# RetNet attention and a bilinear feed-forward: the last block of rows, its groups one after the other, its sums in PSUM banks of their own

## The chip, the cores and the metric

The kernel runs on one core of a Trainium2 chip, as one launch. The metric is the device time of that launch in microseconds (us); lower is better. Before the change three runs took 321.66, 322.04 and 322.22 us; their median is 322.04 us.

## The reference

Eight batches of eight heads, 576 positions, head size 64. Each head's scores are damped by a power of its own gamma, without a softmax, and multiplied into the values. The heads are then laid side by side, which gives 4608 rows of 512 numbers, and a bilinear feed-forward layer follows: two products to 1536 columns, multiplied with each other, and a product back to 512 columns.

```python
scores = scale * (q @ k.T)                       # per batch and head, 576 x 576
D[i, j] = gamma[h] ** (i - j) if i >= j else 0
x = ((scores * D) @ v)                           # heads side by side: 4608 x 512
out = ((x @ w_a) * (x @ w_b)) @ w_out            # 1536 wide inside, 4608 x 512 float32 out
```

## The kernel before, in words

The rows go through the feed-forward in blocks: one of 512, two of 256, and then seven of 512 (`blocks`, L127). The attention of later rows is woven between the matmuls of earlier blocks by a list of jobs with due times (`todo`). By the last block all attention is done; nothing is woven into it but its own work.

For a block of 512 rows, `ffn_block` (L1064) runs twelve steps, one for each 128 of the 1536 inner columns. A step makes `pa` with four matmuls (L1090), ScalarE copies it to `ha` in bf16 (L1101), TensorE makes `pb` with four matmuls (L1108), and VectorE multiplies the two into `hT` (L1113). `row_sums` (L944) then makes sums of pieces of `hT` on VectorE (L952), partly into `hsum` and partly in place.

From row 1536 on, the product with `w_out` is done by `rows_mixed` (L982), with seven products in place of eight of the two-by-two blocks (a scheme of Strassen's kind). A block has two groups of 256 rows, g = 0 and 1. For each group there are seven "ways" of six matmuls (128x256 outputs, L1009), 84 matmuls in a block. The results of one group are gathered from four PSUM areas:

- `straights[g]`: way 3, later with way 6 added, in its first half; way 4, later with way 7 added, in its second half.
- `both[:, g]`: way 1. `crosses[g]`: ways 5 and 2.

Vector work puts them together. `kept("straight", ...)` and `kept("crossed", ...)` are copies on ScalarE (L1019). GpSimd adds the two copies into the middle half of the output tile `osb` (L1038). VectorE makes `less` = way 1 minus `crossed` (L1045), and after ways 7 and 6 it adds `less` to the two halves of `straights[g]`, which gives the outer quarters of `osb` (L1054, two adds of 256 columns for each group).

TensorE takes its instructions in the order in which the program writes them. Before, that is: ways 3 and 4 for both groups, way 1 for both, ways 5 and 2 for group 0, then for group 1, ways 7 and 6 for group 0, then for group 1. `straights[0]`, `straights[1]` and the cross area of group 1 come from the four-bank pool `ps_ffn`; way 1 of both groups and the cross area of group 0 share one two-bank tile `m15`.

The stores: in all blocks but the last they are put off to the next block (`formed`, `store_formed`) and issued by the SP queue. The last block (`closing`) cannot put them off. Its group 0 holds leftover rows of four batches, so `store_mixed` (L959) issues four transfers for it, of 32 tile rows of 4 KB each; they go to the ACT queue. Its group 1 is one piece of 128 tile rows, stored in three parts by the SP queue: the middle half after GpSimd (256 KB), and each outer quarter after its add (128 KB each).

Of the kernel before, what the change touches and what calls it, by code (L numbers as in the profile page):

```python
# [10 lines left out]
FP32 = mybir.dt.float32  # L11
# [3 lines left out]
ALU = mybir.AluOpType  # L15
# [3 lines left out]
def kernel(  # L19
# [10 lines left out]
    nc = tc.nc  # L30
# [14 lines left out]
    NP = NTOK // 256  # L45
# [16 lines left out]
    def place(n):  # L62
        return n if n < NP - 2 else 2 * NP - 3 - n

    def rows_of(n):

        if n not in LEFT:
            b, m = PAIRS[n]
            return [(kp, 0, 128, b, 256 * m + 128 * kp) for kp in (0, 1)]
        return [(i // 2, 64 * (i % 2), 64, 4 * LEFT[n] + i, S - 64)  # L70
                for i in range(4)]

    def pool(name, bufs, space=None):
        kw = {} if space is None else {"space": space}
        return ctx.enter_context(tc.tile_pool(name=name, bufs=bufs, **kw))
# [13 lines left out]
    late, early = {}, ExitStack()  # L89
# [13 lines left out]
    ps_ffn = pool("ps_ffn", 4, PS)  # L103
    opening, ps_sc, ps_o = ExitStack(), {}, {}
# [155 lines left out]
    def pair_tables(step):  # L260
# [6 lines left out]
        else:  # L267
            for h in (2 * step - 2, 2 * step - 1):
# [8 lines left out]
                for n in range(FIRST)]  # L277
    second = sum_pool.tile([128, FIRST, HP, 64], FP32, tag="sums",
                           name="second")
# [28 lines left out]
    def work(budget, up_to=2):  # L308
        jobs.sort(key=lambda job: job[0])
        while jobs and jobs[0][0] <= up_to and jobs[0][1] <= budget:  # L310
            _, cost, job = jobs.pop(0)
            job()
            budget -= cost

    def pass_on(count):
        while copies_due and count:
            copies_due.pop(0)()
            count -= 1
# [610 lines left out]
    WIDE = DM // 2  # L929
# [29 lines left out]
    def store_mixed(G, osb, cols=slice(0, 2 * DM), on=nc.sync):  # L959

        n = place(G)
        for kp, r0, m, b, s0 in rows_of(n):
            if n in LEFT:
                p0 = kp * 64 + r0 // 2
                m //= 2
            elif kp == 1:
                continue
            else:
                p0, m = 0, 128
            rows = out[b * S + s0:b * S + s0 + 2 * m].rearrange(  # L970
                "(p two) c -> p (two c)", two=2)
            on.dma_start(rows[:, cols],
                              osb[p0:p0 + m].rearrange("p k c -> p (k c)")
                              [:, cols])

    formed = []
# [5 lines left out]
    def rows_mixed(tok0, hT, sums):  # L982

        pass_on(math.inf)
        NP2 = NF // 2
        pair = [tok0 // 256 + g for g in (0, 1)]
        closing = NP - 1 in pair
        straights = [ps_ffn.tile([128, 2, WIDE], FP32, tag="ab",
                                 name=f"m34{g}") for g in (0, 1)]
        mixed = ps_o[0].tile([128, 2, 2, WIDE], FP32, tag="o", name="m15")  # L990
        apart = ps_ffn.tile([128, 2, WIDE], FP32, tag="ab", name="m52")
        both, crosses = mixed[:, 0], (mixed[:, 1], apart)

        def product(g, way, ps, begins=True):
            t0 = 256 * g
            to = {1: both[:, g], 2: crosses[g][:, 1], 3: straights[g][:, 0],
                  4: straights[g][:, 1], 5: crosses[g][:, 0],
                  6: straights[g][:, 0], 7: straights[g][:, 1]}[way]
            for p in ps:
                even, odd = 2 * p, 2 * p + 1  # L1000
                rows, cols = {
                    1: (sums[:, 0, p, g], wo_sums[:, 0, p]),
                    2: (hT[:, even, t0 + 128:t0 + 256], wo_sb[:, even, 0:WIDE]),
                    3: (hT[:, even, t0:t0 + 128], wo_sums[:, 3, p]),
                    4: (hT[:, odd, t0 + 128:t0 + 256], wo_sums[:, 4, p]),
                    5: (hT[:, odd, t0:t0 + 128], wo_sb[:, odd, WIDE:]),
                    6: (sums[:, 1, p, g], wo_sums[:, 1, p]),
                    7: (sums[:, 2, p, g], wo_sums[:, 2, p])}[way]
                nc.tensor.matmul(to, rows, cols, start=(begins and p == 0),  # L1009
                                 stop=True, skip_group_check=True)  # L1010
                yield 0.5, False

        osbs = [o_pool.tile([128, 2, DM], FP32, tag="osb", name="osb2")
                for _ in pair]
        flats = [osb.rearrange("p k m -> p (k m)") for osb in osbs]

        def kept(name, own):
            t = late[name].tile([128, 2, WIDE], FP32, tag=name, name=name)
            nc.scalar.copy(t, own)  # L1019
            return t  # L1020

        first, rest = range(NP2 - 1), (NP2 - 1,)
        for part in (first, rest):
            for g in (0, 1):
                yield from product(g, 3, part)
                yield from product(g, 4, part, False)
        kept_straight = [kept("straight", straights[g]) for g in (0, 1)]
        for part in (range(4), range(4, NP2)):
            for g in (0, 1):
                yield from product(g, 1, part, g == 0)  # L1030
        work(math.inf)
        pass_on(math.inf)
        lesses = []
        for g in (0, 1):
            yield from product(g, 5, range(NP2))
            yield from product(g, 2, range(NP2), False)
            crossed = kept("crossed", crosses[g])
            nc.gpsimd.tensor_tensor(  # L1038
                flats[g][:, WIDE:3 * WIDE].rearrange("p (k m) -> p k m", k=2),
                crossed, kept_straight[g], op=ALU.add)  # L1040
            if pair[g] == NP - 1:
                store_mixed(pair[g], osbs[g], slice(WIDE, 3 * WIDE))
            less = late["less"].tile([128, 2, WIDE], FP32, tag="less",
                                     name="less")
            nc.vector.tensor_tensor(  # L1045
                less, both[:, g].unsqueeze(1).to_broadcast([128, 2, WIDE]),
                crossed, op=ALU.subtract)
            lesses.append(less)
        for g in (0, 1):
            yield from product(g, 7, range(NP2), False)  # L1050
            yield from product(g, 6, range(NP2), False)
            for k, at, i in ((1, slice(0, WIDE), 0),
                             (0, slice(3 * WIDE, 4 * WIDE), 1)):
                nc.vector.tensor_tensor(flats[g][:, at], straights[g][:, k],  # L1054
                                        lesses[g][:, i], op=ALU.add)
                if pair[g] == NP - 1:
                    store_mixed(pair[g], osbs[g], at)
            if closing and pair[g] < NP - 1:
                store_mixed(pair[g], osbs[g], on=nc.scalar)
            elif not closing:  # L1060
                formed.append((pair[g], osbs[g]))
        yield 0, True

    def ffn_block(tb, tok0, n, runs):  # L1064
# [62 lines left out]
        if tok0 >= 256 * MIXED:  # L1127
            yield from rows_mixed(tok0, hT, sums)
            return
# [119 lines left out]
    starts, at = {}, 0.0  # L1249
# [89 lines left out]
    at = 0.0  # L1339
# [40 lines left out]
```

## Time and profile before

| | us |
|---|---|
| median of three runs | 322.04 |
| the profiled execution, whole | 322.96 |
| its span, first to last instruction | 321.0 |
| TensorE busy | 312.6 (97% of the span) |
| VectorE busy | 199.7 (62%) |
| ScalarE busy | 145.6 (45%) |
| GpSimd busy | 155.7 (49%) |
| chain that ended last, share on TensorE | 92% |

The profile is one execution of the program. A line of a timeline has the start, the duration, the engine, the line of the kernel, the operation and the tiles; a bracket behind it tells how long the engine sat idle before it and what ended that. PE is TensorE, DVE VectorE, ACT ScalarE, POOL GpSimd; SPq and ACTq are the queues of SyncE and ScalarE that issue transfers. "us to landing" of a transfer runs from its issue to the arrival of its completion. All clock times below are us from the start of the span.

### The profile page before, as it was taken

Reading aid. Unit: us, or ns where it says so; the run is one execution under the profiler, and the core shown is the slowest. Engines: PE = TensorE matmul, PEld = TensorE weight load, DVE = VectorE, ACT = ScalarE, POOL = GpSimd, SP = SyncE. Lnnn points to the kernel's source line nnn. Section 1 sums busy time; section 2 is a strip of 40 time slices with the busy share of each in tenths; the row PEclk is TensorE's granted clock in tenths of the full one; section 3 lists DMA queues with packets and bytes.
Section 4 is the critical chain, followed back from the end, with each engine's and each line's share of the span. In section 5 each row is a group of like instructions: output and inputs, shape, how many; then the busy total and the mean of one; then the engine's idle time right before and its main releaser. Section 6 shows DMA issues by size and latency. Waiting matters only on the chain.

```text
span 321.0 us, 9165 instructions
## 1 busy us (share of the span) xinstructions
PE 312.6 (97%) x3799; PEld 184.3 (57%) x3799; DVE 199.7 (62%) x374; ACT 145.6 (45%) x323; POOL 155.7 (49%) x169
## 2 busy tenths in 40 slices
PE   8999999999999999999999999999999999999992
PEld 3554457768544554548554864476447744764482
DVE  4845347767758563489558854875667566744652
ACT  6745346536435463454464625553436343323330
POOL 3990078564995577573895099408950300030011
PEclk9999999999999999999999999999999999999998
DMA  8999999999989999999999979974330300030004
GB/s 213 255 200 207 256 228 193 183 209 182 196 176 221 223 218 186 233 219 261 199 251 229 172 233 157 178 170 153 73 65 2 133 3 0 2 122 11 1 0 131
DMA packets 144793, 50.92 MB, mean 159 GB/s; under 512 B 126576, under 2 KB 141680, under 8 KB 144752
## 3 DMA queue, kind: packets, MB, share of 16 engines
q1 hardware_dynamic: 138224, 44.84, 70.2%
q0 software_dynamic: 5808, 4.72, 9.4%
q10 hardware_dynamic: 720, 0.79, 0.9%
q8 instruction: 29, 0.48, 0.7%
q14 instruction: 12, 0.10, 0.1%
HBM read 37.75 MB, written 9.44 MB: 147 GB/s over the span
## 4 chain that ended last, share of the span: by engine, by line
PE 92%; DVE 4%; ACT 1%; issue 1%; DVEq 0%
PE pb L1108 29%; PE pa L1090 28%; PE m L1009 15%; PE po L1134 8%; PE w L1159 2%; PE po L913 2%; PE o L744 1%; PE sc L703 1%; PE o L731 1%; PE kv L632 1%; DVE hT L952 1%; PE tp L373 1%; DVE sums L659 1%; DVE hsum L952 1%; PE sc L391 1%
## 5 line engine op out<-in xcount | busy, mean ns | idle before, releaser
L1113 DVE TENSOR_TENSOR hT<-ha,pb 128x512 bf16<-128x512 bf16 (+1 forms) x120 | 75.7, 632 | 79.5 <-PE pb L1108 67.8
L1108 PE MATMUL pb<-xT,wb_sb 128*128 128x512 bf16 (+1 forms) x480 | 111.6, 358 | 0.1
L1090 PE MATMUL pa<-xT,wa_sb 128*128 128x512 bf16 (+1 forms) x472 | 109.9, 358 | 0.0
L1101 ACT CAST ha<-pa 128x512 bf16<-128x512 f32 (+1 forms) x120 | 64.9, 542 | 97.2 <-PE pa L1090 94.7
L1108 PEld LDWEIGHTS <-wb_sb 128*128 128x128 bf16 x480 | 46.8, 98 | 47.6 <-issue 1.9
L1090 PEld LDWEIGHTS <-wa_sb 128*128 128x128 bf16 x472 | 45.0, 98 | 43.1 <-issue 0.2
L1038 POOL TENSOR_TENSOR osb<-crossed,straight 128x512 f32<-128x512 f32 x12 | 15.2, 1271 | 102.8 <-ACT crossed L1019 95.7
L562 POOL TENSOR_TENSOR qkb<-qf,qs 64x1024 bf16<-64x1024 f32 x12 | 22.9, 1911 | 16.1 <-DMA qf<-in_q_dram 11.0
L1009 PEld LDWEIGHTS <-hT 128*128 128x128 bf16 x288 | 28.1, 98 | 4.6 <-issue 0.3
L589 POOL TENSOR_TENSOR vb<-vf,vs 128x1024 bf16<-128x1024 f32 (+1 forms) x17 | 29.1, 1713 | 3.0 <-DMA vf<-in_v_dram 1.4
L1134 PE MATMUL po<-wo_sb,hT 128*128 128x512 bf16 x120 | 27.8, 379 | 0.0
L1009 PE MATMUL m<-wo_sums,hsum 128*128 128x256 bf16 x216 | 25.5, 273 | 0.0
L567 POOL TENSOR_TENSOR qkb<-qf,qs 64x512 bf16<-64x512 f32 x24 | 24.7, 1051 | 0.7
L1009 PEld LDWEIGHTS <-hsum 128*128 128x128 bf16 x216 | 21.1, 98 | 2.4
L952 DVE TENSOR_TENSOR hsum<-hT 128x1024 bf16<-128x1024 bf16 (+1 forms) x36 | 20.5, 596 | 0.2
L578 POOL CAST qkb<-kf 64x1024 bf16<-64x1024 f32 (+1 forms) x17 | 16.6, 976 | 6.6 <-DMA kf<-in_k_dram 5.8
L712 DVE TENSOR_TENSOR sT<-sc,mask 128x512 bf16<-128x512 f32 x30 | 19.8, 681 | 0.0
L659 DVE TENSOR_TENSOR sums<-kv,sums 128x256 f32<-128x256 f32 x44 | 18.6, 422 | 1.4
L582 POOL CAST qkb<-kf 64x512 bf16<-64x512 f32 (+1 forms) x34 | 18.9, 582 | 0.9
L1134 PEld LDWEIGHTS <-hT 128*128 128x128 bf16 x120 | 11.2, 98 | 12.4
L1009 PE MATMUL m<-wo_sb,hT 128*128 128x256 bf16 x144 | 16.9, 273 | 0.1
L1009 PE MATMUL m<-wo_sums,hT 128*128 128x256 bf16 x144 | 16.7, 273 | 0.0
(111 smaller groups left out, 285.9 us busy)
## 6 DMA issues: line engine op xcount, KB each, us to landing
qf<-in_q_dram SPq DMA_DIRECT2D x32, 256.0 KB, 5.2
vf<-in_v_dram SPq DMA_DIRECT2D x32, 256.0 KB, 5.1
kf<-in_k_dram SPq DMA_DIRECT2D x31, 256.0 KB, 4.9
out_dram<-osb SPq DMA_DIRECT2D x9, 512.0 KB, 3.7
out_dram<-osb SPq DMA_DIRECT2D x18, 128.0 KB, 3.3
out_dram<-osb SPq DMA_DIRECT2D x7, 256.0 KB, 3.6
wo_sb<-in_moe_w_out_dram POOLq DMA_DIRECT2D x3, 512.0 KB, 16.0
qf<-in_q_dram SPq DMA_DIRECT2D x8, 128.0 KB, 4.1
```

The lines of the kernel that those rows point to most:

```text
L562: nc.gpsimd.tensor_tensor(per_head(qkb[0:64, Q]), per_head(t[0:64]), by[0:64].unsqueeze(2).to_broadcast([64, 2 * H, D]), op=ALU.mult)
L567: nc.gpsimd.tensor_tensor(per_head(qkb[64:128, Q])[:, 1 - r::2], per_head(t[64:128])[:, r::2], by[64:128, r::2].unsqueeze(2).to_broadcast( ...
L589: nc.gpsimd.tensor_tensor(vb[:, e].rearrange("p (h d) -> p h d", d=D), t[:, e].rearrange("p (h d) -> p h d", d=D), decay[:, at], op=ALU.mult)
L659: nc.vector.tensor_tensor(sums[:, i], own, prev, op=ALU.add)
L712: nc.vector.tensor_tensor(sT[:, on].rearrange("p c k s -> p (c k) s"), sc[on].rearrange("p c k s -> p (c k) s"), mask3.unsqueeze(1).to_bro ...
L952: lambda e=e: nc.vector.tensor_tensor(*e[:3], op=e[3]))
L1009: nc.tensor.matmul(to, rows, cols, start=(begins and p == 0), stop=True, skip_group_check=True)
L1090: nc.tensor.matmul(pa[:, 0:n], wa_sb[:, c, fs], xT[:, c], start=(c == 0), stop=(c == NC - 1))
L1101: nc.scalar.copy(ha[:, 0:n], pa[:, 0:n])
L1108: nc.tensor.matmul(pb[:, 0:n], wb_sb[:, c, fs], xT[:, c], start=(c == 0), stop=(c == NC - 1))
L1113: nc.vector.tensor_tensor(hT[:, F, 0:n], has[F][:, 0:n], pb[:, 0:n], op=ALU.mult)
L1134: nc.tensor.matmul(po, hT[:, F, u * 128:(u + 1) * 128], wo_sb[:, F], start=(F == 0), stop=(F == NF - 1))
```

## The change

Only `rows_mixed` is edited. For all blocks but the last, the program keeps the same instructions in the same order: the code is only rearranged into helpers (`cross`, `lessen`, `add_last`). For the last block:

- TensorE's order becomes: ways 3 and 4 for the first four pairs of group 0, then of group 1, then the rest of group 0; way 1 of group 0; the rest of ways 3 and 4 of group 1; ways 5, 2, 7 and 6 of group 0; then ways 5, 2, 1, 7 and 6 of group 1.
- PSUM: the two halves of `straights[1]` lie in two banks (`m31`, `m41`), way 1 of each group in a bank of its own (`m10`, `m11`, from the pool that held scores), the cross areas in `m520` and `m521`.
- The copy of `straights[1]` is two copies of 256 columns. `less` is made in two instructions of 256 columns.
- Group 0 is stored in whole rows by the SP queue (four transfers) as soon as its adds are done.
- Group 1's middle half is stored by the ACT queue. Its first outer quarter is added and stored after way 7, the other after way 6; both by the SP queue.

```diff
-        straights = [ps_ffn.tile(... name=f"m34{g}") for g in (0, 1)]
-        mixed = ps_o[0].tile([128, 2, 2, WIDE], FP32, tag="o", name="m15")
-        apart = ps_ffn.tile([128, 2, WIDE], FP32, tag="ab", name="m52")
-        both, crosses = mixed[:, 0], (mixed[:, 1], apart)
+        if closing:
+            straights = [bank("m340"), [bank("m31")[0], bank("m41")[0]]]
+            both = [bank(f"m1{g}", ps_sc[0], "sc")[0] for g in (0, 1)]
+            spare = ps_o[0].tile([128, 2, 2, WIDE], FP32, tag="o", name="m521")
+            crosses = [bank("m520"), Halves(spare[:, 0])]
...
+        def cross(g):
+            yield from product(g, 5, range(NP2))
+            yield from product(g, 2, range(NP2), False)
+            crossed[g] = kept("crossed", crosses[g].whole)
+            at = slice(WIDE, 3 * WIDE)
+            nc.gpsimd.tensor_tensor(
+                flats[g][:, at].rearrange("p (k m) -> p k m", k=2),
+                crossed[g], kept_straight[g], op=ALU.add)
+            if pair[g] == NP - 1:
+                store_mixed(pair[g], osbs[g], at, nc.scalar)
+
+        def lessen(g):
...
+            for ks in (slice(0, 1), slice(1, 2)) if closing else (slice(0, 2),):
+                nc.vector.tensor_tensor(lesses[g][:, ks], ...)
+
+        def add_last(g, k, at, i):
+            nc.vector.tensor_tensor(flats[g][:, at], straights[g][k],
+                                    lesses[g][:, i], op=ALU.add)
+            if pair[g] == NP - 1:
+                store_mixed(pair[g], osbs[g], at)
+
+        if closing:
+            for g, ps in ((0, range(4)), (1, range(4)), (0, range(4, NP2))):
+                yield from product(g, 3, ps)
+                yield from product(g, 4, ps, g == 1)
+            kept_straight = {0: kept("straight", straights[0].whole)}
...
+            yield from product(0, 1, range(NP2))
+            for way in (3, 4):
+                yield from product(1, way, range(4, NP2))
+            kept_straight[1] = kept("straight", *straights[1])
+            yield from cross(0)
+            lessen(0)
+            for way, *end in ends:
+                yield from product(0, way, range(NP2), False)
+            for way, *end in ends:
+                add_last(0, *end)
+            store_mixed(pair[0], osbs[0])
+            yield from cross(1)
+            yield from product(1, 1, range(NP2))
+            lessen(1)
+            for way, *end in ends:
+                yield from product(1, way, range(NP2), False)
+                add_last(1, *end)
+            yield 0, True
+            return
```

More of the change, by code (lines that the diff above doesn't have):

```diff
@@ L987, in rows_mixed, with __init__, bank @@
         closing = NP - 1 in pair
-        straights = [ps_ffn.tile([128, 2, WIDE], FP32, tag="ab",
-                                 name=f"m34{g}") for g in (0, 1)]
-        mixed = ps_o[0].tile([128, 2, 2, WIDE], FP32, tag="o", name="m15")
-        apart = ps_ffn.tile([128, 2, WIDE], FP32, tag="ab", name="m52")
-        both, crosses = mixed[:, 0], (mixed[:, 1], apart)
+        class Halves(list):
+            def __init__(self, whole):
+                self.whole = whole
+                super().__init__(whole[:, k] for k in (0, 1))
+        def bank(name, place=ps_ffn, tag="ab"):
+            return Halves(place.tile([128, 2, WIDE], FP32, tag=tag, name=name))
+        if closing:
[3 more added lines that the diff above has]
+            crosses = [bank("m520"), Halves(spare[:, 0])]
+        else:
+            straights = [bank(f"m34{g}") for g in (0, 1)]
+            mixed = ps_o[0].tile([128, 2, 2, WIDE], FP32, tag="o", name="m15")
+            both = [mixed[:, 0, g] for g in (0, 1)]
+            crosses = [Halves(mixed[:, 1]), bank("m52")]
         def product(g, way, ps, begins=True):
             t0 = 256 * g
-            to = {1: both[:, g], 2: crosses[g][:, 1], 3: straights[g][:, 0],
-                  4: straights[g][:, 1], 5: crosses[g][:, 0],
-                  6: straights[g][:, 0], 7: straights[g][:, 1]}[way]
+            to = {1: both[g], 2: crosses[g][1], 3: straights[g][0],
+                  4: straights[g][1], 5: crosses[g][0],
+                  6: straights[g][0], 7: straights[g][1]}[way]
             for p in ps:
@@ L1015, in rows_mixed, with kept @@
         flats = [osb.rearrange("p k m -> p (k m)") for osb in osbs]
-        def kept(name, own):
+        def kept(name, *own):
             t = late[name].tile([128, 2, WIDE], FP32, tag=name, name=name)
-            nc.scalar.copy(t, own)
-            return t
+            width = 2 // len(own)
+            for k, part in enumerate(own):
+                nc.scalar.copy(t[:, width * k:width * k + width], part)
+            return t
+        crossed, lesses = {}, {}
+        ends = ((7, 1, slice(0, WIDE), 0), (6, 0, slice(3 * WIDE, 4 * WIDE), 1))
@@ new lines, in cross @@
+        def cross(g):
[9 more added lines that the diff above has]
+        def lessen(g):
+            lesses[g] = late["less"].tile([128, 2, WIDE], FP32, tag="less",
+                                          name="less")
+            for ks in (slice(0, 1), slice(1, 2)) if closing else (slice(0, 2),):
+                nc.vector.tensor_tensor(
+                    lesses[g][:, ks],
+                    both[g].unsqueeze(1).to_broadcast(
+                        [128, ks.stop - ks.start, WIDE]),
+                    crossed[g][:, ks], op=ALU.subtract)
@@ new lines, in add_last @@
+        def add_last(g, k, at, i):
[8 more added lines that the diff above has]
+            kept_straight = {0: kept("straight", straights[0].whole)}
+            work(math.inf)
+            pass_on(math.inf)
+            yield from product(0, 1, range(NP2))
[17 more added lines that the diff above has]
+            return
@@ L1026, in rows_mixed @@
                 yield from product(g, 4, part, False)
-        kept_straight = [kept("straight", straights[g]) for g in (0, 1)]
+        kept_straight = [kept("straight", straights[g].whole) for g in (0, 1)]
         for part in (range(4), range(4, NP2)):
@@ L1032, in rows_mixed @@
         pass_on(math.inf)
-        lesses = []
         for g in (0, 1):
[L1035 to L1048, printed above, removed]
-        for g in (0, 1):
[L1050 to L1061, printed above, removed]
+            yield from cross(g)
+            lessen(g)
+        for g in (0, 1):
+            for way, *end in ends:
+                yield from product(g, way, range(NP2), False)
+            for way, *end in ends:
+                add_last(g, *end)
+            formed.append((pair[g], osbs[g]))
         yield 0, True
```

## The prediction

> **What bounds the kernel now.** I read the page first. TensorE is busy for 97% of the span and carries 92% of the chain that ended last, so a change that removes no matmul can only gain where TensorE does not set the time. The second place to look is the end.
>
> ```profile
> span 321.0 us, 9165 instructions
> PE 312.6 (97%) x3799; PEld 184.3 (57%) x3799; DVE 199.7 (62%) x374; ACT 145.6 (45%) x323; POOL 155.7 (49%) x169
> PE 92%; DVE 4%; ACT 1%; issue 1%; DVEq 0%
> ```
>
> The chain in order of time, its last pieces:
>
> ```profile
> 305.97 8.71 PE m L1009 x80
> 314.68 0.55 issue
> 315.24 0.42 DVE osb L1054
> 315.66 0.33 DVEq L1375
> ```
>
> The last block's 84 products start at 305.97 (80 of the 84 have records). VectorE is done at 315.99. The span ends at 321.0, so 5.0 us follow in which no engine computes. The waits of the SP queue at the end, and the transfers' list, say what these are:
>
> ```profile
> SPq L1375 <- DMA out_dram<-osb: 2.9, 2, 2.2
> out_dram<-osb ACTq DMA_DIRECT2D x4, 128.0 KB, 3.0
> out_dram<-osb SPq DMA_DIRECT2D x1, 256.0 KB, 2.2
> out_dram<-osb SPq DMA_DIRECT2D x2, 128.0 KB, 3.4
> ```
>
> They are seven stores, 1 MB in all. The timeline of the end:
>
> ```profile
> 306.08 0.69 DVE L1113 TENSOR_TENSOR hT<-ha,pb 128x512 bf16<-128x512 bf16 x1 [0.44 <-PE pb L1108]
> 307.29 1.09 DVE L952 TENSOR_TENSOR hsum<-hT 128x512 bf16<-128x512 bf16 x3
> 308.29 0.75 DVE L952 TENSOR_TENSOR hT<-hT 128x512 bf16<-128x512 bf16 x2
> 311.25 0.58 ACT L1019 COPY crossed<-m 128x512 f32<-128x512 f32 x1 [1.71 <-PE m L1009]
> 311.87 0.69 DVE L1045 TENSOR_TENSOR less<-m,crossed 128x512 f32<-128x512 f32 x1 [2.82 <-ACT crossed L1019]
> 311.97 2.58 POOL L1038 TENSOR_TENSOR osb<-crossed,straight 128x512 f32<-128x512 f32 x2 [27.36 <-ACT crossed L1019]
> 312.36 2.78 PE L1009 MATMUL m<-wo_sums,hsum 128*128 128x256 bf16 x24
> 312.56 0.58 ACT L1019 COPY crossed<-m 128x512 f32<-128x512 f32 x1 [0.72 <-PE m L1009]
> 313.93 0.76 DVE L1054 TENSOR_TENSOR osb<-m,less 128x256 f32<-128x256 f32 x2
> 314.57 2.13 SPq L972 DMA_DIRECT2D out_dram<-osb  x3
> 314.76 1.96 ACTq L972 DMA_DIRECT2D out_dram<-osb  x4
> 315.24 0.75 DVE L1054 TENSOR_TENSOR osb<-m,less 128x256 f32<-128x256 f32 x2 [0.55 <-issue]
> ```
>
> TensorE ends at 312.36 + 2.78 = 315.14 and the last two adds run from 315.24. All seven stores are issued in the 2.2 us from 314.57 on, group 0's too, though it needs only half of the products. In short windows, the second and third stores of the SP queue stand alone, each with its time to landing behind it (the third is the one that ends last):
>
> ```profile
> 315.69 0.35 SPq L972 DMA_DIRECT2D out_dram<-osb  x1
> out_dram<-osb SPq DMA_DIRECT2D x1, 128.0 KB, 3.3
> 316.13 0.57 SPq L972 DMA_DIRECT2D out_dram<-osb  x1
> out_dram<-osb SPq DMA_DIRECT2D x1, 128.0 KB, 3.6
> ```
>
> The last store lands at 316.13 + 3.6 = 319.73; 1.27 us of closing steps follow to 321.0. The table of half-microsecond stretches shows why 128 KB takes 3.6 us where 256 KB took 2.2 (the last two columns are the share of the transfer engines and GB/s):
>
> ```profile
> 315.00:315.50 0.50, 0.14 (x2) 0.00 (x0) 0.26 (x1) 0.00 (x0) 0.00 (x0) 1.00 0.10 41
> 315.50:316.00 0.50, 0.00 (x0) 0.00 (x0) 0.49 (x2) 0.00 (x0) 0.00 (x0) 1.00 1.02 385
> 316.00:316.50 0.50, 0.00 (x0) 0.00 (x0) 0.00 (x0) 0.00 (x0) 0.00 (x0) 1.00 1.24 344
> 316.50:317.00 0.50, 0.00 (x0) 0.00 (x0) 0.00 (x0) 0.00 (x0) 0.00 (x0) 1.00 0.96 164
> 317.00:317.50 0.50, 0.00 (x0) 0.00 (x0) 0.00 (x0) 0.00 (x0) 0.00 (x0) 1.00 0.95 123
> 318.50:319.00 0.50, 0.00 (x0) 0.00 (x0) 0.00 (x0) 0.00 (x0) 0.00 (x0) 0.50 0.91 336
> 319.00:319.50 0.50, 0.00 (x0) 0.00 (x0) 0.00 (x0) 0.00 (x0) 0.00 (x0) 0.50 0.11 33
> ```
>
> ```profile
> q10 hardware_dynamic: 36, 0.08, 95.8%
> ```
>
> The transfer engines are full from about 315.45 (a tenth of the first stretch) to about 319.06 (a tenth of the last). In 316.50 to 317.00 only packets of q10, the ACT queue with group 0, move (the line by queue of that half microsecond). The SP store of 315.69 has not begun a microsecond after its issue. So the end is set by 1 MB of stores that come at once.
>
> **The change part by part.** All terms are counted from the profiled execution (span 321.0, whole 322.96). It lies 0.92 above the median 322.04, so I take the difference over to the median.
>
> Matmuls. There are 84 before and after, of one shape. The 24 of the row at 312.36 last 2.78 us, and 8.71 / 80 gives 0.109 each. With the last end at 315.14, matmul n ends at 315.14 - (84 - n) x 0.109. This fits before: n = 48 ends at 311.22, and the copy starts at 311.25. TensorE ends no earlier unless it now waits, and the new order moves four inputs nearer. The last `hT` (306.77) is first needed by matmul 20, starting at 308.04. The last row sums (`hsum`: its way-1 part, first of three, about 307.7; in place: 309.04) are needed by matmul 25 at 308.6 and matmul 41 at 310.3. Cover is 1.3, 0.9 and 1.3 us; if it were gone each would cost the shortfall. The banks `m31` and `m41` come from an older `pb` and `pa`, freed before 306. `m520` comes from the last `pb` (306.77), used at 309.2. Price: nothing.
>
> Group 0. Its ways 5 and 2 end at n = 42 (310.56): the copy runs 310.60 to 311.18, GpSimd 311.32 to 312.60 (its two adds took 2.58). `less` in two instructions costs what two adds of that size cost, 0.75 where one took 0.69: 311.22 to 311.97. Ways 7 and 6 end at n = 54 (311.87), so the adds run 312.0 to 312.76. Before, they ran 313.93 to 314.69. Group 0 is ready 1.9 us earlier.
>
> Its stores move from the ACT queue to SP. Four such stores of the block before went through SP:
>
> ```profile
> 286.17 0.34 SPq L972 DMA_DIRECT2D out_dram<-osb  x1
> 287.49 0.43 SPq L972 DMA_DIRECT2D out_dram<-osb  x1
> out_dram<-osb SPq DMA_DIRECT2D x4, 128.0 KB, 2.2
> ```
>
> From the first issue to the end of the fourth is 287.92 - 286.17 = 1.75 us, with 2.2 to landing. Here that is 312.80 to 314.55, the last landing at about 316.3, its data moved before 316. The transfer engines are idle until then, so nothing delays them.
>
> Group 1. Ways 5 and 2 end at n = 66 (313.18); the copy runs 313.22 to 313.80, GpSimd 313.94 to 315.21; ACT issues the middle store at 315.23 (before: 314.57 on SP). This store is 0.66 later. Way 1 ends at n = 72 (313.83), `less` runs 313.93 to 314.68. Way 7 ends at n = 78 (314.49), so the first add starts when VectorE is free, 314.72 to 315.14. SP has been free since 314.55; it issues at 315.17. The last add starts where the first of the two started before, 315.24, and ends at 315.66: the last store goes out at 315.69, not 316.13. That is 0.44 gained, safely: the same add, the same queue.
>
> Landing of the last store. The low end is 2.2 (the 256 KB store into idle engines), the high end 3.6 (the row above). Counting bytes: 512 KB instead of 1 MB, from about 316.05 (315.17 and the 0.88 us that passed before between the issue of 314.57 and the busy engines at 315.45), at the 365 GB/s of the first two busy stretches, need 1.4 us: the last byte at 317.45. Before, the engines emptied at 319.06 and the landing was 0.67 later: 318.1. Counting from the low end: 315.69 + 2.2 = 317.9. I take 318.0, near the low end, because the packets that stood ahead of this store before are gone by 316.
>
> The Trainium skill, DMA: Bandwidth & Descriptors, section Queues, rings and completion order, says that the completion mark of a transfer lands only after every earlier write of the same transfer engine, across its queues. By that rule the middle store on the ACT queue holds back the SP store's landing too, and the byte count is the one to use, and the sum would be minus 1.6; no row here separates the two.
>
> Sum: last landing 319.73 to 318.0, minus 1.73, with the closing 1.27 as before. Profiled 322.96 - 1.73 = 321.2; median 322.04 - 1.73 = 320.3.
>
> **The rivals.** A measurement of this kernel can tell about 0.2%, 0.64 us, from no change.
>
> *The small stores are slow by themselves.* The 128 KB stores (1 KB a row) took 3.3 and 3.6 us; if that is their nature and not the queue ahead of them, only the 0.44 of the issue remains, or 0.6 with 3.4: 321.5. For it: no 1 KB-row store in idle engines is in this trace. Against it: in 316.50 to 317.00 these stores did not move at all while q10's did. This would be "no change".
>
> *SP becomes the bound, slower than before.* Six stores stand on one queue, where before three and four went side by side; the last two are queued behind the four of group 0. Their issue has taken longer elsewhere:
>
> ```profile
> L972 SPq DMA_DIRECT2D out_dram<-osb x16: 333/363/1054, 161.2 to 316.1; - x16
> ```
>
> At the largest, four take 4.2 us and the last store goes out at 312.80 + 4.2 + 0.44 = 317.46. With the 3.4 of the two stores it lands at 320.86, 1.13 later than before: 323.2. The slack is 315.17 - 314.55 = 0.6 us, so the price begins at 0.6 us for an issue; the gained 0.44 is lost at 0.72, and slower than before needs about 1.05 and the slow landing together. Against it: the same four took 1.75 in the block before, and their median is 0.363.
>
> The Trainium skill, same page, section Issuing engines are not separate DMA queues, speaks against this part of the change: starting transfers from several engines saves the issuing engine's time. By the rows that time is the 1.75 us and is covered; only without the slack would it count.
>
> *TensorE waits in the new order.* It would need a cover of 0.9 us or more to vanish; nothing in these rows has such spread. It is in the last 1%.
>
> **How the numbers follow.** Forecast (stores spread out, landing between 2.2 and about 3.2): 0.84, 320.3. Slow small stores: 0.10, about 321.5. SP bound: 0.05, up to 323.2; TensorE 0.01. Low end: landing 2.2 gives minus 1.83, and the three runs spread by 0.3 below and 0.2 above their median: rounded up for both, 319.6. The high end takes in the slow small stores, 321.5. Chances: faster 0.84, same 0.10, slower 0.06.
>
> **What would show it.** Right: in the timeline of the changed kernel, four SP stores from about 312.8; the last add still starting at 315.24 and the last store issued near 315.7; transfer engines busy from about 313.7 and empty by about 317.5; a span of about 319.3. Partly wrong: the last store out at 315.7, but 3.3 or more to landing. Wrong: an SP issue that begins more than 0.1 us after its add has ended, or TensorE idle between 306 and 315, so that its last matmul ends after 315.3.

## The result, and the profile after

The changed kernel takes 321.01 us (median of 22 runs, 319.97 to 323.37); the kernel before, run beside it, takes 322.25 us (22 runs, 321.66 to 323.82). The ratio is 0.9962, with a 95% interval from 0.9948 to 0.9977: 1.24 us less, between 0.7 and 1.7. The forecast was 1.73 less, with 319.6 to 321.5 us as its range.

The profiled execution of the changed kernel took 320.63 us in all, 2.33 less than that of before. First its page and the last pieces of its chain:

```profile
span 318.4 us, 9134 instructions
PE 308.0 (97%) x3763; PEld 183.4 (58%) x3799; DVE 198.9 (62%) x376; ACT 145.7 (46%) x324; POOL 155.6 (49%) x169
305.31 9.18 PE m L1022 x84
314.49 0.02 issue
314.51 0.43 DVE osb L1062
```

The page has 36 matmul records fewer than that of before; the second profile of the same program, shown below, has all 3799. So the lower busy time of TensorE is no gain. In the last block all 84 products have records here and take 9.18 us, 0.109 each. The block begins 0.66 us earlier than in the profile of before (305.97). Nothing of the change lies ahead of it: the block began at 305.31 to 306.40 in four profiles of this program. To compare the ends, that has to come off, so I count from the block's first product to the end of the span, and call it the tail: 321.0 - 305.97 = 15.03 us before, 318.4 - 305.31 = 13.09 after. The 0.55 of "issue" in the chain of before is no loss that was won back: four of its matmul records are missing there, and the last adds started 0.10 behind TensorE's end (315.24 and 315.14). Now it is 0.02. The timeline of the end:

```profile
309.93 0.58 ACT L1034 COPY crossed<-m 128x512 f32<-128x512 f32 x1 [0.83 <-PE m L1022]
310.55 0.76 DVE L1055 TENSOR_TENSOR less<-m,crossed 128x256 f32<-128x256 f32 x2 [2.17 <-ACT crossed L1034]
311.30 0.75 DVE L1062 TENSOR_TENSOR osb<-m,less 128x256 f32<-128x256 f32 x2
312.11 3.20 SPq L972 DMA_DIRECT2D out_dram<-osb  x6
312.35 2.13 PE L1022 MATMUL m<-wo_sums,hsum 128*128 128x256 bf16 x18
314.51 0.43 DVE L1062 TENSOR_TENSOR osb<-m,less 128x256 f32<-128x256 f32 x1 [0.15 <-PE m L1022]
314.57 0.35 ACTq L972 DMA_DIRECT2D out_dram<-osb  x1
```

The SP queue now starts at 312.11, 2.38 us ahead of TensorE's end; before, the first store of all went out at 314.57, 0.57 ahead of it. In short windows, the fourth store of group 0 and the last store of all stand alone, and the list of transfers gives their times to landing:

```profile
313.40 0.43 SPq L972 DMA_DIRECT2D out_dram<-osb  x1
314.97 0.35 SPq L972 DMA_DIRECT2D out_dram<-osb  x1
out_dram<-osb SPq DMA_DIRECT2D x6, 128.0 KB, 2.2
out_dram<-osb ACTq DMA_DIRECT2D x1, 256.0 KB, 2.3
out_dram<-osb SPq DMA_DIRECT2D x1, 128.0 KB, 2.3
```

The third row is the median over all six SP stores, the last row that of the store issued at 314.97. It lands at 314.97 + 2.3 = 317.27, and 1.13 of closing steps follow. Before, it needed 3.6. The half-microsecond stretches (last two columns: share of the transfer engines, GB/s) show why:

```profile
313.00:313.50 0.50, 0.50 (x7) 0.45 (x5) 0.23 (x1) 0.13 (x1) 0.23 (x1) 1.00 0.85 197
314.50:315.00 0.50, 0.00 (x0) 0.00 (x0) 0.43 (x1) 0.00 (x0) 0.04 (x1) 1.00 1.05 270
315.50:316.00 0.50, 0.00 (x0) 0.00 (x0) 0.00 (x0) 0.00 (x0) 0.00 (x0) 1.00 1.07 387
316.50:317.00 0.50, 0.00 (x0) 0.00 (x0) 0.00 (x0) 0.00 (x0) 0.00 (x0) 1.00 0.47 162
317.00:317.50 0.50, 0.00 (x0) 0.00 (x0) 0.00 (x0) 0.00 (x0) 0.00 (x0) 1.00 0.00 0
```

The transfer engines already work while TensorE computes (0.85 at 313.0), and are empty by about 316.75, 2.3 us behind TensorE's end (314.49). Before, they were empty at 319.06, 3.9 behind it.

### The profile page after: what moved, and what is told of

It reads as the page before. It is cut to its first block, busy times and chain, and to the rows that moved or that the text cites. A ratio compares the mean times of both kernels' runs of the same rounds, so it can differ in the third digit from the quotient of the medians.

```text
span 318.4 us, 9134 instructions
## 1 busy us (share of the span) xinstructions
PE 308.0 (97%) x3763; PEld 183.4 (58%) x3799; DVE 198.9 (62%) x376; ACT 145.7 (46%) x324; POOL 155.6 (49%) x169
## 4 chain that ended last, share of the span: by engine, by line
PE 90%; DVE 3%; DMA 2%; issue 2%; POOL 1%; SPq 1%; ACT 0%; DVEq 0%; POOLq 0%
PE pb L1159 29%; PE pa L1141 28%; PE m L1022 16%; PE po L1185 8%; DMA vf<-in_v_dram 2%; PE po L913 2%; PE sc L703 1%; PE o L731 1%; PE o L744 1%; SPq L175 1%; PE kv L632 1%; DVE hT L952 1%; POOL vb L365 1%; DVE sums L659 1%; PE pa L902 1%
## 5 line engine op out<-in xcount | busy, mean ns | idle before, releaser
L1141 PE MATMUL pa<-xT,wa_sb 128*128 128x512 bf16 (+1 forms) x448 | 106.4, 356 | 1.9 <-issue 1.2
L1185 PE MATMUL po<-wo_sb,hT 128*128 128x512 bf16 x113 | 26.7, 379 | 0.8 <-issue 0.6
L578 POOL CAST qkb<-kf 64x1024 bf16<-64x1024 f32 (+1 forms) x17 | 15.9, 935 | 8.0 <-DMA kf<-in_k_dram 7.1
```

Of the source, the lines that this page charges most:

```text
L1141: nc.tensor.matmul(pa[:, 0:n], wa_sb[:, c, fs], xT[:, c], start=(c == 0), stop=(c == NC - 1))
L1185: nc.tensor.matmul(po, hT[:, F, u * 128:(u + 1) * 128], wo_sb[:, F], start=(F == 0), stop=(F == NF - 1))
```

## The experiments

The theory was: the end was set by 1 MB of stores in one burst, and the change spreads it. Its first rival was that 128 KB stores with 1 KB a row are slow by themselves, so that only the earlier last issue counts. The first four kernels tell these apart; the second of them edits the kernel before, all others the changed one.

**The changed kernel, a second time.** No edit.

> The changed kernel once more, in five rounds. Theory A (all of the change is in the end of the run: 1.73 forecast; in the two profiles the stretch from the first product of the last block to the end of the span fell from 15.0 to 13.1 us): the stretch from the last block's first product to the end is again 13.1 us, plus or minus 0.2, and what the totals show beyond or below 1.9 us is spread of the time up to the last block. Total 1.2 to 2.0 us below before. Theory B (the change also costs something ahead of the last block, since the medians differ by only 1.2): the last block begins later than 305.97, by about 0.6 us, in this profile too.

Measured: 321.47 us (12 runs), ratio 0.9956 (0.9936 to 0.9977). The comparison repeats; the profile does not. Its chain, a short window on its timeline, the store that ends last, the queue of instruction loads in the list for 312.5 to 313, and two stretches:

```profile
305.38 9.19 PE m L1022 x84
312.55 1.65 SPq L972 DMA_DIRECT2D out_dram<-osb  x1
315.70 0.88 SPq L972 DMA_DIRECT2D out_dram<-osb  x1
q8 instruction: 1, 0.02, 13.1%
313.50:314.00 0.50, 0.50 (x7) 0.44 (x6) 0.50 (x2) 0.00 (x0) 0.50 (x1) 1.00 0.10 17
314.00:314.50 0.50, 0.50 (x6) 0.25 (x3) 0.44 (x2) 0.00 (x0) 0.50 (x1) 1.00 0.03 8
```

The second issue of group 0 takes 1.65 us, and beside it a 16 KB load of instructions (q8) moves. The stores behind it wait on the queue (the four issues take from 312.19 to 315.13, 2.94 us), the transfer engines fall almost idle from 313.5 to 314.5, and the rest comes as a burst again. The last store goes out 1.13 behind TensorE's end (314.57), not 0.48, and the tail is 319.8 - 305.38 = 14.42. So two tails, 13.1 and 14.4, come from one program.

**The kernel before without group 0's last stores.** 512 KB of the output is left out.

```diff
-            if closing and pair[g] < NP - 1:
-                store_mixed(pair[g], osbs[g], on=nc.scalar)
-            elif not closing:
+            if not closing:
                 formed.append((pair[g], osbs[g]))
```

> The kernel before, with the four stores of the last block's group 0 left out (128 rows of leftover positions pair by pair are not written; everything else is as before). Theory A (the last stores are slow because group 0's 512 KB go through the same engines at the same time): the last SP store is issued 1.0 us after the last matmul's end as before, lands 2.2 to 2.5 us after its issue instead of 3.6, and the total falls by 1.1 to 1.4 us. Rival (stores of 1 KB a row are slow by themselves): 3.3 us or more to landing as before, total within 0.3 us of before.

Measured: 320.78 us (6 runs), ratio 0.9936 (0.9912 to 0.996). Its chain and the landing of the three SP stores left (two of 128 KB, one of 256):

```profile
305.26 8.71 PE m L1009 x80
DMA to landing us min/median/max: 1.8/1.8/1.9
```

The same 128 KB stores with 1 KB a row, from the same instructions, land in 1.8 and 1.9 us where they took 3.3 and 3.6. The rival falls: without group 0's stores beside them they are not slow. The tail is 318.6 - 305.26 = 13.34.

**Only the earlier last add.** The new banks and the add and store after each way of group 1, with the products in the old order and the stores on the old queues.

```diff
+            for part in (range(NP2 - 1), (NP2 - 1,)):
+                for g in (0, 1):
+                    yield from product(g, 3, part)
+                    yield from product(g, 4, part, g == 1)
...
-            store_mixed(pair[0], osbs[0])
+            store_mixed(pair[0], osbs[0], on=nc.scalar)
```

> The new PSUM banks and the split last add (first outer quarter added and stored after way 7, the other after way 6), but the old order of the products and the old queues: both groups side by side, group 0's stores on the ACT queue at the end. Theory A: the last SP store is issued 0.45 to 0.55 us after the last matmul's end instead of 1.0, but still takes 3.2 us or more to landing; total 0.3 to 0.7 us below before. Rival (the split add and the banks carry the gain, the stores' order does not matter): the full 1.2 to 1.9 us below before.

Measured: 322.55 us (12 runs), ratio 1.0002 (0.9983 to 1.0021). Chain, last SP store, and the list of transfers:

```profile
305.81 9.18 PE m L1022 x84
315.47 0.41 SPq L972 DMA_DIRECT2D out_dram<-osb  x1
out_dram<-osb ACTq DMA_DIRECT2D x4, 128.0 KB, 3.6
out_dram<-osb SPq DMA_DIRECT2D x2, 128.0 KB, 3.9
```

The last issue does come 0.48 behind TensorE's end (before: 0.99), but the landing grows (the 3.9 is the median of the two SP stores; the last one takes 3.8), and the tail is 14.89, 0.14 less than before. What is issued earlier into a burst waits longer in it: alone, the earlier add is worth nothing that can be measured.

**The changed kernel with group 0 stored late.** Its four transfers go to the ACT queue, behind the middle store.

```diff
-            store_mixed(pair[0], osbs[0])
             yield from cross(1)
+            store_mixed(pair[0], osbs[0], on=nc.scalar)
```

> The changed kernel, except that group 0's four stores are issued by the ACT queue behind group 1's middle store, so at the end instead of 2.4 us ahead of it. Theory A: the two last SP stores are issued as in the changed kernel (0.5 us after the last matmul's end) but take 3.0 us or more to landing, and the four stores, issued until about 1.7 us after the middle one, land last; total 1.2 to 2.2 us above the changed kernel, so about as before. Rival (no contention, only the issue counts): the SP stores land after 2.3 us, and the total is above the changed kernel only by what the four later issues take, 1.2 us at the most.

Measured: 322.56 us (12 runs), ratio 1.0008 (0.9985 to 1.0031), 1.09 above the changed kernel of the same comparison, with a tail of 321.3 - 306.37 = 14.93. The whole gain is gone, with the new order of products and the new banks in place. The expected landing was missed:

```profile
315.63 2.73 ACTq L972 DMA_DIRECT2D out_dram<-osb  x5
out_dram<-osb ACTq DMA_DIRECT2D x4, 128.0 KB, 2.8
out_dram<-osb SPq DMA_DIRECT2D x2, 128.0 KB, 1.9
```

The SP stores got ahead and landed in 1.9; group 0's came last on ACT, the fourth issued at 317.92 and landing in 2.3. What is late has changed places. Whether the bytes or the late issues end the kernel here is not separated: the rival on record, at most 1.2 above the changed kernel, fits the 1.09 better than the theory's 1.2 to 2.2. Either way, the early stores of group 0 are the part that gains.

The next kernels ask about the slow issue of the second profile: what it costs, and what takes it away.

**The instruction load moved.** 24 more matmuls at the start of TensorE's program, so that the loads fall at other places of it.

```diff
-    warm(8, 512)
+    warm(32, 128)
```

> The changed kernel with 24 matmuls more at its start, for the same work there: the eight warming matmuls of 512 columns become 32 of 128, 3.4 and about 3.3 us of TensorE. In the second profile of the changed kernel a 16 KB load of the instruction queue at 312.78 to 313.83 lay beside an SP issue of 1.65 us (312.55 to 314.20); in the first profile that load came after the end and all issues took 0.43 us at most. 24 matmuls more ahead shift the place of such loads in TensorE's sequence by 24 matmuls, here 2.6 us: to about 310.2, ahead of the first SP store. Theory C (that load is what slows the SP issue, and through it the end, in part of the executions): no SP issue of group 0 above 0.5 us, the stretch from the last block's first product to the end is 13.1 us, median 0.4 to 0.7 us below the changed kernel's and the upper half of its executions no longer 1 to 2 us above the lower. Rival (the slow issue has another cause): median and spread as the changed kernel's.

Measured: 322.17 us (12 runs), ratio 0.9975 (0.996 to 0.9989). The list for 312 to 312.5, the chain, and the SP stores of the tile (shortest, median, longest issue in ns; first and last start):

```profile
q8 instruction: 1, 0.02, 15.1%
307.95 9.18 PE m L1022 x84
L972 SPq DMA_DIRECT2D out_dram<-osb x6: 314/386/422, 314.8 to 317.6; - x6
```

The load now comes ahead of the first store (314.8); no issue is slow and the tail is 13.05. By the clock it comes no earlier than elsewhere (about 312.4, not the 310.2 expected): the last block begins 2.6 us later than in the first profile of the changed kernel, so the total says nothing on the end. This is one profile, and in other profiles the load kept clear of the stores without this edit.

**The outer quarters on the ACT queue, the middle on SP.** The last two stores no longer stand behind group 0's.

```diff
-                store_mixed(pair[g], osbs[g], at, nc.scalar)
+                store_mixed(pair[g], osbs[g], at)
...
-                store_mixed(pair[g], osbs[g], at)
+                store_mixed(pair[g], osbs[g], at, nc.scalar)
```

> The changed kernel with the queues of group 1 swapped: its two outer quarters are stored by the ACT queue, its middle half by SP, behind group 0's four. If the slow issue of SP costs time because the last two stores stand behind it in SP's order: the last store goes out 0.5 us after the last matmul's end in every execution, median 0.2 to 0.5 us below the changed kernel's. Rival (a slow issue means slow transfers anyway, so the 1 MB comes out late whatever the queue): within 0.2 us of the changed kernel.

Measured: 321.73 us (9 runs), ratio 0.9959 (0.9943 to 0.9975), among those of the changed program (0.9933 to 0.9966 in four comparisons). In its profile the load came only behind the last store, so no issue was slow, and the last store went out at 315.10, again 0.48 behind TensorE's end (314.62); the tail is 13.26. No gain: it lies 1.07 above the next kernel, which ran beside it and is the changed program over again, with intervals that overlap. And its profile did not meet the case it was made for.

**The last adds written behind way 6.** Meant to put the last issue back where it was.

```diff
             for way, *end in ends:
                 yield from product(1, way, range(NP2), False)
+            for way, *end in ends:
                 add_last(1, *end)
```

> The changed kernel, but both adds of group 1 stand behind way 6, as before the change. Theory A with the 0.44 us of the forecast: the last store goes out 0.9 us after the last matmul's end instead of 0.5 and lands after 2.2 to 2.4 us; total 0.3 to 0.5 us above the changed kernel. Rival (as in the run with the split add alone, the issue time of the last store is worth nothing): within 0.15 us of the changed kernel.

Measured: 320.66 us (6 runs), ratio 0.9933 (0.9917 to 0.9949). Expected was something else, because the edit changes nothing: each engine's instructions are the changed kernel's. The first add starts at 314.18, ahead of TensorE's end at 314.72, wherever the program writes it. In the kernel before, with the same order in the code but both sums in one tile and bank, it started at 315.24, behind TensorE's end at 315.14. So the place in the code is not what lets it start; the separate tiles in separate banks are what differs. This kernel is one more run of the changed kernel: tail 318.6 - 305.54 = 13.06, longest SP issue 430 ns. It also shows how far ratios of one program lie apart: 0.9933 to 0.9966.

**Group 0 early on the ACT queue, the middle store on SP.**

```diff
-                store_mixed(pair[g], osbs[g], at, nc.scalar)
+                store_mixed(pair[g], osbs[g], at)
...
-            store_mixed(pair[0], osbs[0])
+            store_mixed(pair[0], osbs[0], on=nc.scalar)
```

> The changed kernel with group 0's four stores on the ACT queue at their early place, and group 1's middle store on SP, as in the kernel before. By the order of the queues: the ACT engine's copy of group 1's crossed sums stands behind the four issues (1.75 us), so it starts at about 313.9 instead of 312.55 (counted in the profile of the changed kernel); GpSimd and the first add follow about 1.3 us later; on SP the two outer stores stand behind the middle one, which waits for GpSimd. The last store goes out about 1.7 us later than in the changed kernel; total 1.3 to 2.0 us above it. Rival (ACT's issues do not hold up its copies): within 0.3 us of the changed kernel.

Measured: 322.69 us (one run). A short window, the list for 312.5 to 313, and the copy behind the stores:

```profile
312.66 1.32 ACTq L972 DMA_DIRECT2D out_dram<-osb  x1
q8 instruction: 1, 0.02, 12.9%
314.98 0.59 ACT L1034 COPY crossed<-m 128x512 f32<-128x512 f32 x1 [4.33 <-DMA out_dram<-osb]
```

The slow issue appears on the other queue too, so it does not belong to SP. Here the issues hold up arithmetic: ScalarE has to make the crossed copy of group 1 behind its four issues, and starts it at 314.98; the second profile of the changed kernel has that copy at 312.62. The tail is 321.0 - 305.44 = 15.56, in one run, so the cost is not known, but the place is clear.

**Group 0 on two queues.** Its first two transfers go to SP, the other two to ACT between the crossed copy and the middle store, so that two stand on each queue (`which`, new in `store_mixed`, picks the transfers).

```diff
             crossed[g] = kept("crossed", crosses[g].whole)
+            if closing and g == 1:
+                store_mixed(pair[0], osbs[0], on=nc.scalar, which=(2, 3))
...
-            store_mixed(pair[0], osbs[0])
+            store_mixed(pair[0], osbs[0], which=(0, 1))
```

> The changed kernel with group 0's four stores on two queues: the first two on SP as now, the other two on the ACT queue, between ScalarE's copy of group 1's crossed sums and the middle store, so from about 313.2. In two profiles an issue that lay beside a 16 KB load of the instruction queue took 1.65 and 1.32 us; in four without such a load beside it, none of group 0's took over 0.43. Theory C (this slow issue, and the three behind it on SP, are what makes the end later in part of the executions): with two issues on SP the queue is free before 314.4 even so, the last store goes out 0.5 us after the last matmul, the stretch from the last block's first product to the end is 13.0 to 13.5 us with or without the load, and the median is 0.3 to 0.7 us below the changed kernel's of the same call. Rival (the spread comes from ahead of the last block): median within 0.25 us of the changed kernel's.

Measured: 320.72 us (6 runs), ratio 0.9936 (0.9912 to 0.9959). Chain, a slow issue, the last store, the list for 312.8 to 313.2, and the ACT stores (shortest, median, longest issue in ns):

```profile
305.78 9.18 PE m L1025 x84
312.95 1.52 SPq L975 DMA_DIRECT2D out_dram<-osb  x1
315.44 0.35 SPq L975 DMA_DIRECT2D out_dram<-osb  x1
q8 instruction: 1, 0.02, 19.0%
L975 ACTq DMA_DIRECT2D out_dram<-osb x3: 357/359/960, 313.1 to 315.0; - x3
```

Beside the load an issue on SP took 1.52 us again, and the second of the two on ACT 0.96; both ended at about 314.47. But the last store still goes out 0.48 behind TensorE's end (314.96), and the tail is 319.0 - 305.78 = 13.22. The slow issues cost nothing that shows here: no other store of group 0 stood behind them on its queue, and both queues were free before the stores of group 1 were due.

**The changed kernel, a third time,** beside the kernel on two queues.

> The changed kernel again, to compare the next two with on the same chip, and as one more profile of it: with a load of the instruction queue beside the SP issues the stretch from the last block's first product to the end is 14 us or more, without it 13.1, by theory C; by the rival there is no such tie. Total 1.0 to 1.9 us below before.

Measured: 321.58 us (12 runs), ratio 0.9966 (0.9948 to 0.9984), 0.86 above the kernel on two queues, though the intervals overlap. In its profile the load came behind the end of the span, the longest issue took 431 ns, and the tail is 319.6 - 306.40 = 13.2.

**The changed kernel without group 0's stores.** 512 KB of the output is left out.

```diff
-            store_mixed(pair[0], osbs[0])
             yield from cross(1)
```

> The changed kernel without group 0's four stores in the last block (128 rows pair by pair are not written). SP has nothing to issue before the two outer quarters. Theory C: no slow issue can come, the end is the same in all executions (about 12.7 to 13.0 us from the last block's first product), the median 0.5 to 0.9 us below the changed kernel's and the spread of the spans about half of it. Rival (the spread comes from ahead of the last block, or from transfers that are slow at all events): the spread of the spans is as wide as the changed kernel's, and the median lies at most 0.4 us lower, by the shorter landing.

Measured: 320.84 us (9 runs), ratio 0.9949 (0.993 to 0.9968), 0.74 below the changed kernel beside it. The tail is 318.6 - 305.28 = 13.32 (12.7 to 13.0 was expected), so where no issue is slow, group 0's 512 KB is hidden entirely (13.1 to 13.2 with it). The 0.74 would then be what the executions with a slow issue add; the intervals overlap, so that is not shown. And a slow issue is not all of the spread: the spans here go from 318.6 to 320.1, three of nine above 319.6, with no issue of group 0 left to be slow (318.4 to 320.9 in the changed kernel beside it).

This kernel also tells what the earlier last issue is worth with group 0 out of the way, beside the kernel before without group 0's last stores. The SP stores there, then the last store here and the landings of its three:

```profile
L972 SPq DMA_DIRECT2D out_dram<-osb x3: 350/354/383, 313.9 to 315.4; - x3
314.94 0.35 SPq L972 DMA_DIRECT2D out_dram<-osb  x1
DMA to landing us min/median/max: 1.9/2.3/2.3
```

There the last store goes out at 315.4, 1.0 behind TensorE's end (314.43), and lands in 1.9; here it goes out 0.5 behind the end (314.47) and takes 2.3. Both land at about 317.3, and the tails are 13.34 and 13.32: the earlier issue is given back in the landing here too. The middle store goes out later here (314.54, there 313.87); that this is the reason is not shown.

**Group 0 on two queues, a second time.**

> The version with group 0's four transfers on two queues (first two on SP, other two on ACT between the crossed copy and the middle store), a second time. Theory C (beside the instruction load an early issue is slow; with two transfers on each queue the last issue stays 0.5 us behind the last add, whether the load comes early or late): ratio 0.992 to 0.9955 to the kernel before, first product of the block to end of span 13.0 to 13.4, spans of the runs within about 1 us. Rival (its first measurement was luck; the two queues make no difference to the end): ratio 0.9955 to 0.998 as the changed kernel's own runs, spans spread over 2 to 3 us.

Measured: 321.22 us (6 runs), ratio 0.9948 (0.993 to 0.9967). Spans of 318.4 to 319.5 and a tail of 318.5 - 305.36 = 13.14, with the load behind the end. By the ratio the two queues can't be told from the changed kernel (0.9933 to 0.9966 in its four comparisons). By the spans there is a weak sign: none of the 12 runs on two queues is above 319.5, while 20 of the 52 runs of the changed program are above 319.6 (up to 321.7), though none of the six of the kernel with the last adds behind way 6. But spans above 319.6 also come where no issue of group 0 can be slow (the kernel without its stores), so they do not tell of that issue alone. I would take it for the better version, but no difference is shown.

## Why the prediction was right, and where not

*What bounds the end.* Right, and shown from both sides: with 512 KB left out of the burst the landing falls from 3.6 to 1.9 and the tail by 15.03 - 13.34 = 1.69, and with group 0 stored late again the gain is gone.

*Matmuls and group 0.* Right. With 0.66 taken off for the earlier block, the copy was forecast for 309.94 (measured 309.93), `less` for 310.56 (310.55), the adds for 311.34 (311.30), the first store for 312.14 (312.11). The four issues took 313.83 - 312.11 = 1.72 (forecast 1.75). TensorE's end moved with its start (0.65 earlier): no wait.

*Group 1.* Middle store forecast for 314.57 (314.57), last store for 315.03 (314.97), landing 2.3 (2.3). The sum of minus 1.73 stands beside a tail of minus 1.94 in that profile: 0.51 from the issue, 1.3 from the landing, 0.14 from the closing steps.

*"That is 0.44 gained, safely".* This is the step that failed. The issue came earlier by that much in every profile where the queue was free, but it is no term of its own. With the burst left as it was, the landing took it back (3.8 us, ratio 1.0002); with group 0 left out of both kernels it did so again (tails of 13.34 and 13.32). No run shows it to be worth anything, and taking group 0 out of the burst gave 1.69 without it. So the gain is group 0's, and the split of the sum into issue and landing only says where the time stands in one profile; that both of its terms came out as forecast does not show that either is a gain by itself. And it isn't safe: behind one slow issue the last store went out 1.13 after TensorE's end, later than the 0.99 of before.

*The rivals.* Small stores slow by themselves: refuted. SP as the bound: half right. Its place was right, and so was its point, if the 0.6 us for an issue is read as a mean of the four, 2.4 in all: they took 2.94 in the second profile, and the last store waited. One issue over 0.6 does not do it (1.52 on two queues). The row it went by, 1.054 us at most (a 512 KB store at 161.21), was too short, since 1.65 was seen. Its size was too large: the tail of 14.42 is still 0.61 less than before, since only one of the four issues is slow. I had it as a separate case of 1 in 20. It came in one of four profiles of the changed program. Their tails (13.09, 14.42, 13.06, 13.2) average 13.44, which is 1.59 less than the one profile of before: by this estimate the slow issue takes some 0.35 off the 1.94 of the first profile. The rest, down to the measured 1.24, lies within the interval of 0.7 to 1.7 and the spread of 1.1 us in where the block begins, and stays open.

Two slips in the working: with the 3.4 of the slow landing the kernel would be as slow as before from 0.77 us for an issue (312.80 + 4 x 0.77 + 0.44 + 3.4 = 319.72), not from about 1.05; and the lowest of the three runs lay 0.38 below their median, not 0.3. Neither changes the range.

The Trainium skill, DMA: Bandwidth & Descriptors, section Issuing engines are not separate DMA queues, has it that starting transfers from several engines saves the time of the one that issues. The prediction let this count only without the slack. The runs agree: with 1.65 us the slack was gone on one queue (tail 14.42), and with the issues shared between two engines 1.52 us cost nothing that shows (13.22). On the completion mark, the prediction's other point from the Trainium skill, the runs don't decide.

## What to carry to other kernels

Where the last transfers are slow, ask what stands ahead of them before asking about their form: the last store took 1.9, 2.3 and 3.8 us by what else was in flight. Store what is ready early while TensorE still works, and don't add up the gains of one path: here the landing took back what an earlier issue had won, with a full burst and without group 0. Where several issues stand ahead of the one that ends the kernel, give each queue no more of them than the slack covers at the slowest issue seen (one profile here shows it to hold; a shorter time is not shown), and look at several profiles, since one may show none that is slow.

## What was not expected of the hardware

Outside a full burst an issue of a store of 32 tile rows takes 0.31 to 0.44 us, but beside a 16 KB load of instructions it took 1.65, 1.52 (both SP) and 1.32 (ACT): in all three profiles in which the load met such an issue ahead of the end of the products; beside the 1.52, one on ACT took 0.96. In the six profiles with group 0 stored early where the load came earlier or later, the longest took 0.44. Loads are not the only cause of a longer issue: in a full burst, 0.90 us was seen without one beside it in the kernel with group 0 stored late, and 1.16 in the kernel with only the earlier last add.

```profile
316.00 1.16 ACTq L972 DMA_DIRECT2D out_dram<-osb  x1
```

That the load is the cause of the slow issue, and how, isn't shown: the two came together in these three profiles, and no run takes the load away and leaves the rest as it is. Nor is it shown why the load comes at about 312.8 in one execution and at about 319.6, behind the end of the span, in another of the same program.
